# Gate, up and query rows in half the width, the mean after the MLP from sums of w_down's rows, and a new order of loads for a two-layer decode step

## The chip, the cores and the metric

The kernel runs on one core of a Trainium2 chip. The metric is the device time of one execution in microseconds. Shown are the median of three runs and one profiled execution with its trace.

## The reference

One decode step for four tokens through attention, a gated MLP, and both once more with the same weights and the same caches.

```python
def _A_ref(x, k_cache, v_cache, wq, wo):        # x (4, 1, 512); caches (4, 8, 4096, 128)
    q = (x @ wq) as 32 heads of 128
    k, v = each of the 8 cached heads for 4 query heads
    p = softmax(q @ k.T * 128 ** -0.5)
    return (p @ v) as one row of 4096 @ wo
def _B_ref(x, w_gate, w_up, w_down):            # (512, 1792), (512, 1792), (1792, 512)
    return (sigmoid(x @ w_gate) * (x @ w_up)) @ w_down

x = A_x
x = x + _A_ref(_layernorm(x), A_k_cache, A_v_cache, A_wq, A_wo)
x = x + _B_ref(_layernorm(x), B_w_gate, B_w_up, B_w_down)
x = x + _A_ref(_layernorm(x), A_k_cache, A_v_cache, A_wq, A_wo)
x = x + _B_ref(_layernorm(x), B_w_gate, B_w_up, B_w_down)
```

All inputs are bf16. K and V of one token and all 8 heads are 8.4 MB each, 67 MB for four tokens, and both layers need them; the ring below holds 14.7 MB of them at a time.

## The kernel before

**Units and half tiles.** The work is cut into 16 units `bhl`: token b, half hg of the 8 cached heads (four heads s), layer l. A unit reads 8 half tiles of K and 8 of V, each 512 KB: one head s, one half q of the 4096 positions. SBUF has a ring of 28 slots (`SLOTS`), each for one half tile. `UNITS` gives the order of the units: `000 010 011 100 001 110 200 111 210 101 211 300 310 201 311 301`. Layer 1 of a token can start only when both of its layer-0 units are done and the token has passed its MLP.

**Loads.** `LOADS` is the order of all loads on SP's queue, written out: a word is a weight (`wq0`, `wo3`, `wg`) or K or V, the unit, and a letter: `a` to `d` a head's both halves in one transfer of 1 MB into two neighbouring slots, `e` to `h` its first half, `i` to `l` its second half, a digit two single halves. A half tile of layer 1 that LOADS doesn't name is kept: the tile of layer 0 stays in its slot until layer 1 has used it. Before, 80 of the 128 half tiles of layer 1 are kept: 23 of token 0, 21 of token 1, 16 of token 2, 20 of token 3. A load waits until the readers of its slot's last tile are done; the wait stands on SP's queue, in order, so the loads behind it wait too.

**A unit.** K tiles are transposed in place on DVE (L896), then PE makes the scores (L904) in `S_ps`. `unit_probs` makes the softmax: maximum on DVE (L928), exponential on ACT (L949), a transpose (L955), 16 products that turn the probabilities (L960), copies to `pt_sb` (L970). `unit_values` multiplies with V (L1003), copies the result (L1025, L1033), adds the parts up (L1056), scales into `oT` (L1078, L1082). In layer 0 PE then multiplies with w_o (L1108).

**The chain of a token.** Between its layers each token has a chain of small steps (`chain`). `gate_up` multiplies one row of x with w_gate and w_up (L1217): 4 column groups of 448 in 4 strips of the array. `gated` makes the tanh on ACT (L1249), the gated product (L1258) and its transpose (L1268) on DVE, in two cuts (`CUTS`: 4 and 10 of 14 pieces of 32 columns). `down` multiplies with w_down, 56 products (L1288). Two DVE steps add the result to x (L1321). The mean of x is a product with a constant (L1330), its copy (L1333), the variance (L1335, L1197), and `rstd` on POOL (L1205). `gated` keeps its values in the slot of a tile that layer 1 loads anew (`LENT`, one word for each chain), which is held from the tanh to the last down product.

**The queries of layer 1** (`queries`) multiply x, which still has its mean in it, with w_q (L826): 16 products of 512 columns, four rows in `Q_ps`. ACT copies them (L835), 4 products turn them (L840), DVE takes off the mean times the column sums of w_q (L846), 16 products on the unit matrix spread them into the scores' layout (L855), DVE masks them into `zq` (L869). `column_sums` makes these sums once (L783, L792).

**The end.** The last unit's w_o product (L1438) and MLP are made for all four tokens at once (`last_part`, `last_chain`), with cuts of 6, 2 and 6 pieces (`LAST_CUTS`); the up product's second part goes to `O_ps`.

**The order on the engines.** All steps are put into a `_Plan`. `schedule` walks through time with a cost for each step, a rank (the load's place, moved by `SHIFTS` for each stage) and a model of the load queue (`DMA_RATE`, `DMA_LAG`, `DMA_SPREAD`), and so gives each engine a fixed order and each load its slot. Where PE would idle it puts constant products in between (`filler`, L1553). The device follows that order, whatever its own times are.

Of the kernel before, what the change touches and what calls it, by code (L numbers as in the profile page):

```python
# [5 lines left out]
dt = mybir.dt  # L6
# [11 lines left out]
DMA_LAG = 1.4  # L18
DMA_SPREAD = 0.2
DMA_START = 1.9  # L20
PATIENCE = 6.201
# [9 lines left out]
CUTS = "0 4 14"  # L31
LAST_CUTS = "0 6 8 14"
PAIRS = "02"
GROUPS = "1441441444214244"
HEADS = "2212222122222222"
LENT = "V00031 V20030 V10110 V21111 V20110"
CHAIN = -3108.651
PROJECT = 2584.665
KEPT_K = -953.257
KEPT_V = -2637.133  # L40
REST_V = 88.299
SHIFTS = {'c0': 81.66, 'c2': -0.1, 'd1': -11.9, 'd2': -26.55, 'd3': 76.83, 'm0': 8.0, 's': 77.55, 'z0': -0.3, 'z16': 4.38, 'z8': 30.04, 'z12': 50.86, 'q0': -15.2, 'v0.1': 92.64, 'o0.1': -4.74, 'w0.1': 248.14, 'k1.0': 4.46, 'p1': 45.85, 'k2.0': -9.73, 'k2.1': -29.77, 'v2.0': -5.96, 'o2.1': -101.79, 'd0': 5.31, 'q3': 51.38, 'k3.1': -52.81, 'p3': 23.58, 'v3.1': -25.26, 'k4.0': -0.08, 'k4.1': 17.87, 'p4': 24.28, 'v4.1': -24.56, 'k5.0': 19.47, 'k5.1': 3.74, 'p5': -17.71, 'v5.0': -8.59, 'v5.1': 34.03, 'w5.1': -6.54, 'p6': -80.04, 'o6.0': -17.29, 'w6.1': -3.83, 'k7.1': 8.14, 'v7.1': -5.26, 'o7.1': -29.48, 'k8.0': -34.2, 'k8.1': 17.95, 'p8': 6.04, 'v8.0': 9.7, 'o8.0': -79.15, 'v8.1': -48.83, 'p9': -1.07, 'v9.1': -42.81, 'o9.1': 15.12, 'w9.1': 1.54, 'k10.1': 20.55, 'v10.0': -41.15, 'o10.0': 9.85, 'w10.0': 36.93, 'w10.1': -3.91, 'k11.0': 7.83, 'k11.1': 36.1, 'v11.0': -4.55, 'v11.1': -2.06, 'k12.1': 314.91, 'v12.0': -16.87, 'o12.0': 1.68, 'w12.0': -0.97, 'q13': 19.97, 'k13.0': 8.85, 'k13.1': -1.52, 'p13': 139.58, 'o13.0': 113.53, 'o13.1': 4.81, 'q14': 42.47, 'k14.1': 1.8, 'p14': -41.58, 'v14.1': 15.08, 'o14.1': 8.19, 'k15.0': 1.08, 'p15': 22.58, 'v15.1': -5.53, 'o15.1': 8.17, 'end': 93.62, 'm1': -11.57, 'k9.0': 3.6, 'w9.0': -21.96, 'k14.0': -6.21, 'c1': 140.82, 'k1.1': 22.57, 'g0': 4.64, 'p2': 0.84, 'o3.1': 18.77, 'v6.0': 2.8, 'v6.1': 0.53, 'q7': -42.76, 'v7.0': 20.84, 'v9.0': -119.56, 'n2': 30.1, 'w11.1': 12.47, 'v13.0': -0.64, 'm3': -25.74, 'v14.0': -1.05, 'k0.1': -45.97, 'p0': 102.93, 'q1': 2.86, 'v1.0': -18.16, 'w3.1': -27.61, 'q5': 12.61, 'w5.0': 9.87, 'g1': -13.65, 'k7.0': 3.96, 'q8': -81.66, 'w8.0': -3.75, 'w8.1': -1.25, 'k9.1': 0.11, 'm2': -13.04, 'q10': -18.43, 'p11': -11.23, 'w11.0': -1.15, 'w12.1': 6.19, 'k0.0': 68.44, 'q2': 66.34, 'v2.1': -36.47, 'v4.0': -8.75, 'o5.0': 32.07, 'o6.1': -88.15, 'h2': 12.76, 'k10.0': -23.93, 'o10.1': -2.79, 'o11.0': -25.41, 'o12.1': 30.81, 'h3': 13.66, 'q15': 3.29, 'o15.0': 2.09, 'z24': -1.06, 'o0.0': -6.06, 'o1.0': 5.71, 'w1.0': 9.25, 'v3.0': -6.6, 'o3.0': -26.33, 'o4.0': -29.01, 'k6.0': 37.29, 'o8.1': -47.34, 'k12.0': 6.65, 'p12': 57.66, 'v12.1': -18.06, 'w0.0': -12.21, 'v1.1': 68.17, 'o1.1': 38.85, 'n0': 10.09, 'h0': 9.25, 'o5.1': -51.91, 'k6.1': 42.17, 'h1': -4.92, 'p7': 48.17, 'o7.0': -24.25, 'o9.0': -10.3, 'g2': 1.73, 'p10': -2.59, 'q11': -13.05, 'v13.1': 117.04, 'g3': 39.19, 'o14.0': -0.78, 'v15.0': 19.07}
PUT_OFF = -380.691
UNITS = "000 010 011 100 001 110 200 111 210 101 211 300 310 201 311 301"
LOADS = "V000a V000d V010g wq1 K010b V010b K000d K000a wq0 V010k K000b wo1 K010a K010k V000c K000c V010a K010g K010d wu V000b wo3 wo0 V010d wo2 wg wd K100g K100h V011j K011j K100l V100e K100i K001a K100e K100b K001d K100k V001f K110d V100i V100b V100d K110c K110b K110a V001d V100k K200d K200c V100g K200a K200b V110e V110i V110b V110d V110c V200c V200h V200l V2000 V2001 K210l K210k K210g K210a V111l K210h K101g K101d K210b V210b K101e V210a K300c V210d V210c V101j V101i V101d V101g V101k K300b K310a K310c K300a K300d V300a K201e K310b K310d V300c V300d V300b V310b V310a V310c V310d K201f K201h K301g K201g K201j K201i K2013 V201i V201f V201e V201j K301f V201c K301k V201d V311d V301e V301b V301c V301h V301l"
# [389 lines left out]
def bass_interleave_layers__gqa_block_cached__glu_gated_glu__decode_kernel(nc, A_x, A_k, A_v, A_wq, A_wo, B_x, B_wg, B_wu, B_wd, out):  # L435
# [14 lines left out]
    FB = FS // 32  # L450
    TH = T // 2
# [52 lines left out]
    small = sb_low("small", [P, 76], bf)  # L504
    xT = small[:, 0:16].rearrange("p (b k) -> p b k", b=B)
    q2, sel = small[:, 16:32], small[:, 32:36]
    sel_o = small[:, 40:72].rearrange("p (t n) -> p t n", t=4)
    ob = q2
    real = sb("real", [P, 80])
    stat = sb_low("stat", [P, 24])  # L510
    col_sum = sb_low("col_sum", [P, 2 * HG])
    mean_of = sb_low("mean_of", [P, B])
    minus = sb_low("minus", [P, 2], bf)[:, 0:1]
    more = sb_low("more", [P, 25])
# [59 lines left out]
    S.put("pool", lambda e: e.memset(minus, -1.0), writes=["minus"], cost=0.1)  # L574
    const("sel", sel, 0.0, [(sel, NE, 1.0, 0, [[-32, 4]])])
# [10 lines left out]
    const("sel_o", small[:, 40:72], 0.0, [  # L586
# [127 lines left out]
    def rank_v(u, pr):  # L714
# [19 lines left out]
        reads=["ones"] + [f"xsum{b}" for b in range(B)], writes=["U", "Uz"], cost=0.35, pairs=2,  # L734
    )
    less_b = U_ps[:, 0:4].unsqueeze(2).broadcast_to([P, B, KD])
    for o, key in ((xT, "xT"), (xc, "xc")):
# [8 lines left out]
        reads=["ones"] + [f"xsq{b}" for b in range(B)], writes=["U"], cost=0.35, pairs=2,  # L746
# [29 lines left out]
    def column_sums(hg):  # L776
        S.stage = f"c{hg}"
        r = max(place["wq0"], place["wq1"]) + 25.0
        for c0 in range(0, HG, 4):
            fns = []  # L780
            for c in range(c0, c0 + 4):
                for k in range(KD):
                    fns.append(lambda e, c=c, k=k: e.matmul(  # L783
                        Q_ps[:, c * WIDE:(c + 1) * WIDE], lhsT=wq[:, k, hg * HC + c * DH:hg * HC + (c + 1) * DH],
                        rhs=minus.broadcast_to([P, WIDE]), start=(k == 0), stop=(k == KD - 1),
                    ))
            S.put(
                "pe", fns, reads=["wq0", "wq1", "Qz", "minus"], writes=[own("Q", c0 == 0)], rank=r, columns=len(fns) * 4 * WIDE,
                lock="Q" if c0 == 0 else None,
            )  # L790
        S.put(
            "dve", lambda e: e.tensor_copy(col_sum[:, hg * HG:(hg + 1) * HG], Q_ps[:, bass.ds(0, HG, step=WIDE)]),  # L792
            reads=[own("Q")], writes=[f"cs{hg}"], cost=0.2, rank=r, free="Q",
        )

    q_out = Q_ps[:, 0:64].rearrange("p (s n h) -> p s n h", n=NQ, h=R)

    def queries(i, rank):
# [797 lines left out]
```

## Time and profile before

| | |
|---|---|
| median of three runs | 285.12 us (284.92 to 286.09) |
| profiled execution | 282.97 us |
| its span, first to last instruction | 281.1 us |
| busy: PE, DVE, ACT, POOL | 217.4, 174.0, 63.5, 10.7 us |
| read from HBM | 106.17 MB |
| load queue on SP | 106.18 MB in 115 K and V transfers and 9 of weights |
| mean granted TensorE clock | 0.988 |

In the rows of the profile an instruction group reads: line, engine, operation, written tile <- read tiles, shapes, count | busy us, mean ns of one | idle time of the engine before them and what ended it. `SPq` rows are issues on the load queue; a wait of SP names the instruction whose end let the load go. PE's busy time holds the constant products.

### The profile page before, as it was taken

To read this page: it belongs to the slowest core of one execution; us is meant where nothing else is said; L and a number is where in the kernel's file an instruction comes from. 1 tells how busy PE (TensorE), PEld (TensorE's weight loads), DVE (VectorE), ACT (ScalarE), POOL (GpSimd) and SP (SyncE) were. 2 spreads that over 40 slices of the span, in tenths; PEclk is the share of its full clock that TensorE was granted. 3 is DMA by queue.
4 is the path that set the end of the run, shared out by engine and by line. 5 is a ranking of instruction groups with operands and counts; after the bars stand their busy time and mean duration, and the time that the engine had idled before them with its cause. 6 is when DMAs were issued, how large, how long until landed. Compare 5 with 4: busy or idle time off the path is not lost.

```text
span 281.1 us, 8157 instructions
## 1 busy us (share of the span) xinstructions
PE 217.4 (77%) x3572; PEld 112.2 (40%) x3612; DVE 174.0 (62%) x387; ACT 63.5 (23%) x155; POOL 10.7 (4%) x40
## 2 busy tenths in 40 slices
PE   1000786988889688999889886898889789989796
PEld 1000444444543343434355441355424454544464
DVE  4036379747268897858623788635999517975222
ACT  1000100052122105002132240332132312233611
POOL 5200000000000000000000000000000000000000
PEclk9999997999999999999999997999999999999999
DMA  7999999999998999999999999999999999989910
GB/s 266 429 422 426 385 417 417 411 380 397 420 369 322 417 385 427 415 416 418 420 412 387 354 419 423 415 413 422 419 417 419 423 408 366 349 293 404 421 61 3
DMA packets 21538, 106.69 MB, mean 380 GB/s; under 512 B 2048, under 2 KB 4096, under 8 KB 13056
## 3 DMA queue, kind: packets, MB, share of 16 engines
q1 hardware_dynamic: 21440, 106.18, 94.3%
q8 instruction: 28, 0.46, 0.7%
q14 instruction: 6, 0.05, 0.0%
q10 hardware_dynamic: 64, 0.01, 0.0%
HBM read 106.17 MB, written 0.00 MB: 378 GB/s over the span
## 4 chain that ended last, share of the span: by engine, by line
DMA 50%; PE 27%; DVE 10%; SPq 7%; issue 3%; ACT 1%; POOL 0%; ACTq 0%; DVEq 0%
DMA slots<-in_A_k_cache_dram 27%; DMA slots<-in_A_v_cache_dram 17%; PE S_ps L904 8%; DMA wd<-in_B_w_down_dram 7%; DVE slots L896 7%; SPq L659 4%; PE O_ps L1003 4%; PE G_ps L1288 2%; PE PT_ps L1553 2%; SPq L668 2%; PE G_ps L1553 2%; PE Q_ps L826 2%; PE M_ps L1056 1%; PE G_ps L1217 1%; PE M_ps L1349 1%
## 5 line engine op out<-in xcount | busy, mean ns | idle before, releaser
L896 DVE STREAM_TRANSPOSE slots<-slots 128x1024 int32<-128x1024 int32 x84 | 100.6, 1222 | 24.8 <-DMA slots<-in_A_k_cache_dram 24.0
L904 PE MATMUL S_ps<-slots,zq 128*32 128x512 bf16 x512 | 62.0, 401 | 7.5 <-DVE slots L896 5.3
L1003 PE MATMUL O_ps<-slots,pt_sb 128*16 128x512 bf16 x504 | 35.9, 380 | 6.2 <-DMA slots<-in_A_v_cache_dram 4.0
L1553 PE MATMUL PT_ps<-wq 128*128 128x512 bf16 (+1 forms) x123 | 33.8, 378 | 2.9 <-issue 2.7
L904 PEld LDWEIGHTS S_ps<-slots,zq 128*32 128x32 bf16 x512 | 19.7, 96 | 35.2 <-DVE slots L896 11.5
L1033 ACT ACTIVATE slots<-O_ps 128x512 bf16<-128x512 f32 (+1 forms) x26 | 15.5, 595 | 47.7 <-PE O_ps L1003 47.7
L760 PE MATMUL Q_ps<-small,wq 128*128 128x4 bf16 x128 | 3.6, 165 | 22.8 <-DMA wq<-in_A_wq_dram 22.8
L1553 PEld LDWEIGHTS PT_ps<-wq 128*128 128x128 bf16 x155 | 12.5, 98 | 19.7 <-issue 12.1
L1003 PEld LDWEIGHTS O_ps<-slots,pt_sb 128*16 128x16 bf16 x504 | 10.6, 87 | 18.3 <-ACT pt_sb L970 4.4
L1108 PEld LDWEIGHTS M_ps<-oT,wo 128*128 128x128 bf16 x512 | 14.7, 97 | 6.5 <-DVE oT L1082 2.9
L1108 PE MATMUL M_ps<-oT,wo 128*128 128x32 bf16 x512 | 16.0, 176 | 1.1 <-DVE oT L1082 0.7
L928 DVE TENSOR_REDUCE small<-S_ps 128x1 f32<-128x512 f32 x16 | 11.0, 687 | 8.7 <-PE S_ps L904 5.6
L970 ACT ACTIVATE pt_sb<-PT_ps 128x256 bf16<-128x256 f32 x32 | 10.5, 381 | 13.0 <-PE PT_ps L960 12.8
L1205 POOL TENSOR_TENSOR stat<-real,small 128x1 f32<-128x1 f32 x8 | 4.4, 549 | 233.1 <-ACT real L1201 233.1
L760 PEld LDWEIGHTS Q_ps<-small,wq 128*128 128x128 bf16 x128 | 3.5, 100 | 23.3 <-DMA wq<-in_A_wq_dram 22.9
L1056 PE MATMUL M_ps<-small,slots 128*64 128x4 bf16 (+2 forms) x204 | 9.7, 176 | 2.8 <-DVE oT L1082 1.3
L1056 PEld LDWEIGHTS M_ps<-small,slots 128*128 128x128 bf16 (+1 forms) x204 | 7.1, 103 | 11.4 <-issue 5.0
L1553 PE MATMUL G_ps<-wq 128*128 128x512 bf16 (+1 forms) x35 | 11.0, 435 | 0.6 <-issue 0.3
L949 ACT ACTIVATE p_sb<-S_ps,pt_sb,stat 128x512 bf16<-128x512 f32 x8 | 7.5, 935 | 16.5 <-DVE pt_sb L942 13.2
L770 ACT ACTIVATE oT<-Q_ps 128x64 bf16<-128x64 f32 x2 | 0.9, 448 | 43.5 <-PE Q_ps L760 43.5
L955 DVE STREAM_TRANSPOSE p_sb<-p_sb 128x256 int32<-128x256 int32 x16 | 7.0, 439 | 5.3 <-ACT p_sb L949 5.2
L869 DVE TENSOR_TENSOR zq<-Q_ps,real 128x256 bf16<-128x256 f32 x16 | 6.4, 400 | 6.1 <-ACT oT L770 5.5
(146 smaller groups left out, 222.9 us busy)
## 6 DMA issues: line engine op xcount, KB each, us to landing
slots<-in_A_v_cache_dram SPq DMA_DIRECT2D x32, 1024.0 KB, 11.1
slots<-in_A_k_cache_dram SPq DMA_DIRECT2D x29, 1024.0 KB, 10.9
slots<-in_A_v_cache_dram SPq DMA_DIRECT2D x28, 512.0 KB, 11.8
slots<-in_A_k_cache_dram SPq DMA_DIRECT2D x26, 512.0 KB, 7.6
wq<-in_A_wq_dram SPq DMA_DIRECT2D x2, 2048.0 KB, 18.5
wo<-in_A_wo_dram SPq DMA_DIRECT2D x4, 1024.0 KB, 22.0
wu<-in_B_w_up_dram SPq DMA_DIRECT2D x1, 1792.0 KB, 23.9
wg<-in_B_w_gate_dram SPq DMA_DIRECT2D x1, 1792.0 KB, 17.0
```

What stands on the lines that cost most here:

```text
L659: return e.dma_start(o, src)
L760: fns.append(lambda e, c=c, k=k: e.matmul(Q_ps[:, c * B:(c + 1) * B], lhsT=wq[:, k, hg * HC + c * DH:hg * HC + (c + 1) * DH], rhs=xT[:, :, k],
L896: "dve", lambda e, t=t: e.transpose(ring[t.slot].bitcast(dt.int32), ring[t.slot].bitcast(dt.int32)),
L904: fns.append(lambda e, s=s, t=t, nn=nn, q=q: e.matmul(S_ps[qi][32 * s:32 * s + 32, :], lhsT=window(qi, s * NQ + nn, q), rhs=ring[t.slot].r ...
L928: dve(lambda e: e.tensor_reduce(ml[at], bank, AX.X, ALU.max, negate=True), [f"S{qi}s{s}" for s in ss], keys("ml", ss), 0.7)
L949: lambda e: e.activation(p_sb[at].rearrange("p (t j r) -> p t r j", j=32, r=2), bank.rearrange("p (t r j) -> p t r j", r=2, j=32), ACTF.Ex ...
L970: "act", lambda e, pr=pr: e.activation(pt_sb[:, (2 * i + pr) % 3], PT_ps[:, 256 * pr:256 * pr + 256], ACTF.Copy),
L1003: fns.append(lambda e, m=m, at=at, v=v, c=c, q=q, pt=pt, bank=bank, x0=x0, x1=x1: e.matmul(bank[m:m + 16, x0:x1], lhsT=pt[:, at:at + 16], ...
L1033: lambda e, lent=lent, rows=rows, o_ps=o_ps, rows_of=rows_of, cols=cols: e.activation(ring[lent.slot][rows, 0:cols], rows_of(o_ps[rows, 0: ...
L1056: return e.matmul(o, lhsT=turned[:, tt * P + at:tt * P + at + n], rhs=heads(tt), start=(tt == 0), stop=(tt == 3))
L1108: fns.append(lambda e, k=k, n=n, h0=h0: e.matmul(M_ps[:, k * WIDE:(k + 1) * WIDE], lhsT=wo[:, h0 + n, k * P:(k + 1) * P], rhs=oT[:, b, h0 ...
L1553: return lambda e: e.matmul(ps_of[:, 0:width], lhsT=wq[:, 0, 0:P], rhs=wq[:, 0, 0:width], start=True, stop=True)
```

## The change

Gate and up are made in two halves of the columns: 8 and 6 of the 14 pieces, stacked as two rows of each strip, so that the elementwise steps are 256 columns wide and not 448. The same is done with the query rows (two rows of 256 and not one of 512). For this x stands in `xz` with zeros on both sides, and each product takes two of the columns. The 4 products that turn the query rows and the 16 that spread them become 32 products that do both. x in `xT` now has its mean off already, by a sum over the gated values with the sums of w_down's rows (14 new reductions on DVE, `chain_sums`); `column_sums` goes. The mean's product stands inside the last cut's `down`, after two of its four groups. The variance is made on DVE (`squares`) and not on ACT. The planner's costs of some small steps change, as do its shifts, and LOADS, LENT, GROUPS and HEADS are new. The words of the new LOADS name 174 half tiles where there were 176, with token 0 keeping 25 where it kept 23; 54 loads are of 1 MB and 66 of 512 KB, where there were 61 and 54. The weights come in the order wo3 wq0 wq1 wo2 wo1 wo0 wd wg wu, where it was wq1 wq0 wo1 wu wo3 wo0 wo2 wg wd.

```diff
-DMA_LAG = 1.4
-DMA_SPREAD = 0.2
+DMA_LAG = 1.55
+DMA_SPREAD = 0.5
...
-CUTS = "0 4 14"
-LAST_CUTS = "0 6 8 14"
+CUTS = "0 2 8"
+LAST_CUTS = "0 4 8"
...
-GROUPS = "1441441444214244"
+GROUPS = "1421442441412144"
...
-LENT = "V00031 V20030 V10110 V21111 V20110"
+LENT = "K00001 V20020 V11101 K20130 V30120"
...
-LOADS = "V000a V000d V010g wq1 K010b V010b K000d K000a wq0 ... V010d wo2 wg wd K100g K100h V011j K011j K100l V100e ..."
+LOADS = "K010d K000d K000f K010j wo3 K010c wq0 K000c V000j K000a wq1 ... wo0 wd V010a V010k wg wu K100f K001i V100g K001j K100d ..."
...
 # queries, layer 1
             for k in range(KD):
                 fns = []
                 for s in range(NS):
-                        fns.append(lambda e, k=k, s=s: e.matmul(
-                            Q_ps[32 * s:32 * s + 1, :], lhsT=xT[:, b, k:k + 1], rhs=wq[:, k, hg * HC + s * 512:hg * HC + (s + 1) * 512],
-                            start=(k == 0), stop=(k == KD - 1),
+                    for a in range(2):
+                        fns.append(lambda e, k=k, s=s, a=a: e.matmul(
+                            Q_ps[32 * s:32 * s + 2, 0:256], lhsT=xz[:, b, k, 1 - a:3 - a],
+                            rhs=wq[:, k, hg * HC + s * 512 + 256 * a:hg * HC + s * 512 + 256 * a + 256],
+                            start=(k == 0 and a == 0), stop=(k == KD - 1 and a == 1),
                         ))
...
+            for nn in range(NQ):
+                for h in range(2):
+                    at = h * DH + 64 * (nn // 2) + nn % 2
+                    for a in range(0, P, 32):
+                        fns.append(lambda e, nn=nn, h=h, at=at, a=a: e.matmul(
+                            q_out[a:a + 32, :, nn, bass.ds(h, 2, step=2)], lhsT=p_sb[:, bass.ds(at, 32, step=2)], rhs=sel,
+                            start=True, stop=True,
+                        ))
...
 # gate_up
+            for a, end in ((0, c1), (1, min(c1, FB - FW))):
+                for j in range(4) if end > c0 else ():
+                    fns.append(lambda e, j=j, a=a, end=end: e.matmul(
+                        dealt(o_ps, (c0, end))[32 * j:32 * j + 2 * nb], lhsT=rows_of(k, a),
+                        rhs=w[:, k, j * FS:(j + 1) * FS].rearrange("p (i m) -> p i m", m=FB)[:, :, FW * a + c0:FW * a + end],
+                        start=(k == 0 and a == 0), stop=(k == KD - 1), skip_group_check=True,
+                    ))
...
 # chain, after the gated cuts
+        weighted(
+            lambda: turned(home).rearrange("p (m i) -> p m i", i=64)[:, :, 0:4], w_sums[:, 8:24].rearrange(pairs, r=4),
+            ..., part_sum[:, 1:2],
+            [f"th{home.name}cd{c0}" for c0, c1 in cuts(CUTS)] + ["wd_sums"], ["part1"], rank,
+        )
+            down(
+                cut, 1, G_ps, "G", rank, home,
+                (lambda: mean_part(U_ps[:, 1:2], part_sum[:, 1:2], ["part1"], rank, True, True)) if cut[1] == FW else None,
+            )
+                out=rest1, in0=U_ps[:, 1:2].broadcast_to([P, KD]), scalar=rs, in1=xc1, op0=ALU.mult, op1=ALU.subtract
...
 # chain_sums
-        for key, at, count, rows in (("wo", 0, 8, lambda n: wo[:, H - 8 + n, :]),):
+        for key, at, count, rows in (("wo", 0, 8, lambda n: wo[:, H - 8 + n, :]), ("wd", 8, FB, lambda n: wd[:, n, :])):
...
 # last_part
+            "pool", lambda e: e.memset(small[:, 0:48], 0.0), writes=[f"xT{b}" for b in every_b], cost=0.1, rank=rank - 4.0,
```

More of the change, by code (lines that the diff above doesn't have):

```diff
@@ L774, in first_q @@
         )
[L776 to L794, printed above, removed]
     q_out = Q_ps[:, 0:64].rearrange("p (s n h) -> p s n h", n=NQ, h=R)
@@ L876, in queries @@
             ),
[L877 removed]
+            reads=[own("Q"), by_key], writes=[f"qz{qi}"], cost=0.41, rank=rank, free="Q",
         )
```

235 lines of the change are left out of this document (108 added, 127 removed).

## The prediction

> **What bounds the kernel now.** I read the page's head, the DMA part and the shares of the chain that ended last; then a table of windows for the rate of the load stream; then, where the rate is low, SP's queue and the chain.
>
> ```profile
> span 281.1 us, 8157 instructions
> q1 hardware_dynamic: 21440, 106.18, 94.3%
> DMA 50%; PE 27%; DVE 10%; SPq 7%; issue 3%; ACT 1%; POOL 0%; ACTq 0%; DVEq 0%
> ```
>
> The load queue moved 106.18 MB and was busy for 94.3% of the span, and half of the last chain is DMA. The kernel is a stream of loads with a tail behind it. The windows show where the stream ran thin (columns: length, busy time of PE, PEld, DVE, ACT, POOL, granted clock, DMA share, GB/s).
>
> ```profile
> 10.00:30.00 20.00, 0.46 (x17) 0.46 (x18) 7.11 (x6) 0.00 (x0) 0.00 (x0) 1.00 1.01 423
> 105.00:130.00 25.00, 22.50 (x263) 9.90 (x264) 18.47 (x31) 5.34 (x13) 0.00 (x0) 1.00 1.01 421
> 60.00:80.00 20.00, 16.98 (x323) 9.44 (x319) 9.83 (x32) 5.08 (x12) 0.55 (x1) 1.00 1.03 404
> 75.00:90.00 15.00, 13.63 (x198) 6.43 (x201) 9.47 (x19) 2.94 (x9) 1.10 (x2) 1.00 0.92 347
> 150.00:160.00 10.00, 8.66 (x194) 5.06 (x185) 5.87 (x15) 3.09 (x9) 0.61 (x2) 1.00 0.97 353
> 235.00:255.00 20.00, 18.22 (x309) 8.80 (x309) 16.41 (x41) 6.55 (x19) 1.10 (x2) 1.00 0.92 331
> 267.50:281.10 13.60, 11.10 (x238) 7.56 (x239) 4.03 (x20) 2.53 (x7) 0.55 (x1) 1.00 0.06 21
> ```
>
> An undisturbed stretch runs at 421 GB/s. Against that, 75 to 90 us lacks 15 x 74 = 1.11 MB, which is 2.6 us of loading; 150 to 160 lacks 0.68 MB, 1.6 us; 235 to 255 lacks 1.80 MB, 4.3 us. These are the stretches of the chains of tokens 0, 1 and 3: while a token is between its layers, its kept tiles hold their slots. The loads end near 267.5 us and 13.6 us of tail follow.
>
> So three things move the end: the bytes, the three dry spells, and the tail.
>
> The first dry spell: SP's waits and issues, two windows of 1 us, and the chain there (start, us, what):
>
> ```profile
> SPq L427 <- PE G_ps L1288: 13.2, 1, 13.2
> 64.56 1.18 SPq L659 DMA_DIRECT2D slots<-in_A_k_cache_dram  x2
> 65.84 0.52 SPq L659 DMA_DIRECT2D slots<-in_A_v_cache_dram  x1
> 66.40 14.91 SPq L659 DMA_DIRECT2D slots<-in_A_k_cache_dram  x2
> 84.54 0.33 SPq L659 DMA_DIRECT2D slots<-in_A_v_cache_dram  x1
> 85.24 4.60 SPq L659 DMA_DIRECT2D slots<-in_A_k_cache_dram  x6
> ...
> 85.00:86.00 1.00, 0.98 (x17) 0.33 (x16) 1.00 (x2) 0.00 (x0) 0.00 (x0) 1.00 0.53 82
> 86.00:87.00 1.00, 0.98 (x20) 0.33 (x16) 1.00 (x2) 0.00 (x0) 0.00 (x0) 1.00 0.91 369
> 60.24 18.97 DMA wd<-in_B_w_down_dram
> 79.35 1.56 PE G_ps L1288 x56
> 85.18 1.13 PE S_ps L904 x14
> ```
>
> Behind w_d (landed by 79.3) four half tiles were issued by 66.4; the next waited 13.2 us for the first chain's down products, whose lent tile held the slot. These four are the 28 slots less 23 kept halves of token 0 less the lent one. The next came at 84.5, after the first scores of unit 100 had freed a slot, and a row of six from 85.2, as layer 1's first scores (85.18) began; the stream ran at 82 GB/s from 85 to 86 and at 369 in the next us, so data flows some 1.5 us after an issue.
>
> **The change, part by part.** The prices are in these rows and the ones behind them.
>
> ```profile
> L896 DVE STREAM_TRANSPOSE slots<-slots 128x1024 int32<-128x1024 int32 x84 | 100.6, 1222 | 24.8 <-DMA slots<-in_A_k_cache_dram 24.0
> L1382 DVE TENSOR_REDUCE more<-wo x8: 676/686/687, 62.6 to 68.4; 128x1 f32<-128x512 bf16 x8
> L783 PE MATMUL Q_ps<-minus,wq 128*128 128x32 bf16 x128 | 3.5, 176 | 3.1 <-DVE col_sum L792 3.1
> L970 ACT ACTIVATE pt_sb<-PT_ps 128x256 bf16<-128x256 f32 x32 | 10.5, 381 | 13.0 <-PE PT_ps L960 12.8
> L835 ACT ACTIVATE p_sb<-Q_ps 128x512 bf16<-128x512 f32 x8 | 4.8, 598 | 15.4 <-PE Q_ps L826 13.7 <-PE PT_ps L960 1.8
> L1258 DVE SCALAR_TENSOR_TENSOR p_sb<-slots,U_ps 128x128 bf16<-128x128 f32 x4 | 1.1, 280 | 7.4 <-ACT slots L1249 7.4
> L1258 DVE SCALAR_TENSOR_TENSOR p_sb<-slots,U_ps 128x320 bf16<-128x320 f32 x4 | 1.9, 484 | 0.0
> L1258 DVE SCALAR_TENSOR_TENSOR p_sb<-slots,stat,O_ps 128x192 bf16<-128x192 f32 x1 | 0.4, 377 | 0.0
> L1268 DVE STREAM_TRANSPOSE slots<-p_sb 128x64 int32<-128x64 int32 x4 | 1.2, 291 | 0.1
> L1268 DVE STREAM_TRANSPOSE slots<-p_sb 128x160 int32<-128x160 int32 x4 | 1.8, 456 | 0.1
> L1268 DVE STREAM_TRANSPOSE slots<-p_sb 128x96 int32<-128x96 int32 x2 | 0.7, 349 | 0.0
> ```
>
> *Bytes.* The words of LOADS sum to 176 half tiles before and 174 after. A half is 0.524 MB, at 421 GB/s 1.25 us: two save 2.5 us of loading. Both are kept by token 0 (23 kept become 25; the others stay at 21, 16 and 20).
>
> *What that takes from the first chain.* With 25 kept and one lent, 2 slots are left instead of 4. Cover behind the last weight falls from four transfers to two, 2.5 us less. The last weight is now w_up, not w_d, with the same bytes ahead of it (30.7 MB), so it lands at the same 79.3. Behind it come the up products, the gating and the last 40 down products, where before there were 56 down products: up 0.93, first cut 0.28 + 0.23, second 0.38 + 0.35, 40 x 26 ns = 1.1, hand-overs 0.3, so about 3.6 against 1.6 us. The queries that follow are about 0.9 shorter (below). So layer 1's first scores come at about 86.3 instead of 85.2. My timeline: two halves last until 81.8; the lent slot is freed near 83.2 and, 1.5 us later, data flows at 84.7; that half and one in a slot freed by unit 100's first scores last to 87.2; the next slots come free near 87.0 and flow at 88.5. That is 2.9 + 1.3 = 4.2 us dry where the window had 2.6: 1.7 us more, rounding up. Ends: nothing, if unit 100's tiles turn over faster; 3.5 us (the two lost transfers and 1 us of later scores), if no slot of unit 100 comes free early. I take 1.7, nearer the row that shows a slot of unit 100 coming free at 84.54.
>
> *Narrow gate, up and queries.* A chain's columns on PE stay the same (448 become 256 + 192, in twice the matmuls). The elementwise steps shrink: the cuts of 128 and 320 columns become 64 and 192, so the products go from 280 + 484 to about 280 + 377 ns and the transposes from 291 + 456 to about 233 (the rows' slope) + 349 ns, 0.27 us together. The copy of the query rows falls from 598 to the 381 ns of a 256-wide copy, 0.22 us.
>
> The up products and the query's way to the scores' layout (token 1):
>
> ```profile
> 149.29 0.93 PE L1217 MATMUL U_ps<-wu,small 128*1 128x448 bf16 x16
> ...
> 154.66 0.38 PE L1330 MATMUL U_ps<-stat 128*128 128x1 f32 x2
> 155.51 0.26 PE L840 MATMUL Q_ps<-small,p_sb 128*128 128x4 bf16 x4
> 155.88 0.23 DVE L846 SCALAR_TENSOR_TENSOR small<-col_sum,mean_of,Q_ps 128x16 bf16<-128x16 f32 x1 [2.02 <-PE Q_ps L840]
> 156.29 0.27 PE L855 MATMUL Q_ps<-small,ident 128*32 128x16 bf16 x16
> ```
>
> From 155.51 to 156.56 are 1.05 us with two hand-overs. 32 products of L855's form replace them: 16 took 0.27, of which 0.17 is the latency of one, so 6.7 ns each, and 32 take 0.38. That saves 0.67. Against that, the mean's two matmuls (0.31 of issue; L1330's pair, which stood after or among the query rows) now stand inside the down products, ahead of x. Twice the matmuls cost some 0.14. A chain is 0.27 + 0.22 + 0.67 - 0.31 - 0.14 = 0.7 us shorter. Chain 0 has this counted above. Chain 2 has no dry spell. Chains 1 and 3 have 1.6 and 4.3 us dry, and I take 0.5 of each: K transposes of 1.22 us sit ahead of the chain's steps on DVE and will eat some. Ends: 0 and 1.4 for both.
>
> [...]
>
> *w_d sums.* 14 reductions of L1382's 686 ns, 9.6 us of DVE, behind w_d, which now lands near 66.7 (5.3 MB ahead of the last weight). DVE was busy 9.83 of 20 us from 60 to 80, of which L1382's w_o sums took 5.5 between 62.6 and 69; these move early, as w_o's last quarter is now the fifth load (DVE has 7.11 busy of 20 between 10 and 30). From 66.7 to 80.8, when the gated products need them, there are 14 us with some 3 busy. I cost them at nothing; three fewer K tiles are transposed (3.7 us). If the cover is gone, x waits for the mean, and each us late is a us dry: 0 to 2.
>
> *Column sums.* 128 products on PE (3.5 us) and two copies go, ahead of the first chain, which waits for its weights: nothing. The loads now begin with K, and the second half of w_q lands after 12.1 MB instead of 11.0: the first products start 2.6 us later under a full load queue, nothing, up to 1 if slots then run short. Twelve more single-half transfers add issue time on SP, which runs ahead: nothing, up to 0.3. The extra memsets on POOL stand ahead of their uses: nothing.
>
> *The tail.*
>
> ```profile
> 274.95 0.39 PE U_ps L1217 x16
> 275.75 0.41 DVE L1258 SCALAR_TENSOR_TENSOR p_sb<-slots,stat,U_ps 128x192 bf16<-128x192 f32 x1 [1.17 <-ACT slots L1249]
> 276.89 1.55 PE L1288 MATMUL G_ps<-slots,wd 128*128 128x32 bf16 x56
> ```
>
> Gating began at 275.75 and the first down product came at 276.89, after the transposes of the first two cuts. With cuts of 128 columns: product 0.28, transpose 0.29, so down starts near 276.35, and its 56 products run on without a gap (the second cut ends near 276.95, the first one's 32 products near 277.2). That is 0.55 us earlier; ends 0 and 0.7.
>
> *Sum.* The profiled execution took 282.97 (281.1 in the span, 1.9 around it): 282.97 - 2.5 + 1.7 - 1.0 - 0.55 = 280.6. The median shown, 285.12, is 2.15 above that execution, so 282.8 for the median.
>
> **Rivals.**
> *More than forecast.* The first dry spell doesn't grow: 282.8 - 1.7 = 281.1, to 280.7 with all of both chains' 0.7. For it: slots of unit 100 did come free during the chain. Against: half the free slots are gone. 0.18.
>
> *The gain is eaten where it is made.* The first spell grows by 3.5: 284.6, the same. For it: 13.2 us of SP's wait there hung on one lent slot. Two transfers saved cost two transfers of cover. [...]
>
> *Slower: w_d's sums late.* The sums end after the first chain's gating. xT now waits for the mean, so each us late is a us more dry. It is the same beyond 0.9 us late (283.7) and slower beyond 3.8 (286.6); all 9.6 us behind the gating would give 292. DVE's 10 idle us from 60 to 80 speak against it. 0.07.
>
> *Slower: the new order itself.* Every load and step has a new place. A new spell as long as the one at 235 to 255 (4.3 us) would give 287.1; it decides from 3.8. 0.12. The profile can't show it.
>
> **How the numbers follow.** About 0.5% (1.4 us) can be told from no change, so faster ends at 283.7 and slower begins at 286.5. Forecast 0.38, and 0.18 for more: faster 0.56. Same: 0.25. Slower: 0.19. For 8 in 10 the range runs from 279.8 (the fuller gain with 0.7 more where the new order closes part of 235 to 255) to 286.8; the forecast's own is 281.1 to 283.7.
>
> **What would show it.** The load queue at 105.1 MB. 75 to 90 us thinner than 347 GB/s (about 300), with SP waiting for L1288 or first scores behind two halves; 150 to 160 and 235 to 255 fuller by 0.5 us each. The 32 products in about 0.4 us. From the last load to the end 13 us. Wrong if the first spell is not thinner, if the mean's matmuls wait for w_d's sums, or if a stretch that is full now runs dry.

## The result, and the profile after

The changed kernel takes 288.09 us (median of 17 runs, 286.18 to 290.72) where the kernel before, run beside it, takes 285.30 (283.66 to 286.46): a ratio of 1.0087, 95% interval 1.0065 to 1.0110. (The ratio leaves out the two slow executions of the changed kernel, 290.56 and 290.72: it is 287.79 over 285.30.) It is slower; faster by 2.3 us was forecast. The profiled execution took 286.65 us, its span 284.4 against 281.1: 3.3 us more. The page's head, the load queue and the shares of the chain that ended last:

```profile
span 284.4 us, 8832 instructions
q1 hardware_dynamic: 22160, 105.13, 92.2%
PE 41%; DMA 38%; SPq 8%; DVE 7%; issue 3%; ACT 2%; ACTq 0%; DVEq 0%
```

The queue moved 1.05 MB less, as planned, and was busy for a smaller share of a longer span. Loads are 38% of the last chain where they were 50%: more time is waited for something else. Windows of the changed kernel, in the columns used above, the last one the tail:

```profile
75.00:95.00 20.00, 19.34 (x416) 12.00 (x420) 11.90 (x41) 3.08 (x11) 1.10 (x2) 1.00 0.65 237
80.00:82.00 2.00, 2.00 (x41) 1.02 (x37) 0.00 (x0) 0.90 (x3) 0.56 (x1) 1.00 0.22 88
86.00:88.00 2.00, 1.84 (x57) 1.04 (x46) 1.21 (x2) 0.45 (x2) 0.55 (x1) 1.00 0.79 256
150.00:165.00 15.00, 13.13 (x330) 8.58 (x332) 4.95 (x27) 2.72 (x8) 1.10 (x2) 1.00 0.88 333
230.00:255.00 25.00, 24.04 (x459) 14.23 (x463) 16.98 (x45) 4.79 (x13) 1.05 (x2) 1.00 0.98 381
271.70:284.40 12.70, 10.12 (x272) 7.56 (x268) 3.33 (x18) 2.27 (x6) 0.55 (x1) 0.95 0.04 12
```

and three of the same windows of the kernel before:

```profile
75.00:95.00 20.00, 16.59 (x251) 7.80 (x254) 12.83 (x25) 5.16 (x14) 1.10 (x2) 1.00 0.94 364
150.00:165.00 15.00, 13.17 (x281) 7.51 (x272) 9.97 (x26) 4.40 (x13) 0.61 (x2) 1.00 0.99 374
230.00:255.00 25.00, 22.75 (x377) 11.16 (x378) 18.40 (x47) 7.15 (x20) 1.10 (x2) 1.00 0.94 345
```

Each spell is (421 less the rate) times the length over 421. The first, of chain 0, was 20 x 57 / 421 = 2.7 us and is 20 x 184 / 421 = 8.7: 6.0 us more. Chain 1's went from 1.7 to 3.1, 1.5 more before rounding. Chain 3's went from 4.5 to 2.4, 2.1 less. With 2.5 us for the bytes and 0.5 for the tail (from 267.9 to the end it was 13.2 us, from 271.7 it is 12.7) this makes 6.0 + 1.5 - 2.1 - 2.5 - 0.5 = 2.4 of the 3.3 us. Of the rest, 0.4 us is already there at 80 us (395 GB/s over the first 80 us, where it was 397); the remainder lies spread over the other stretches.

So nearly all of the loss is in one place. There SP's queue shows (start, us):

```profile
50.16 0.50 SPq L668 DMA_DIRECT2D wd<-in_B_w_down_dram  x1
60.25 0.81 SPq L659 DMA_DIRECT2D slots<-in_A_v_cache_dram  x2
61.10 0.43 SPq L668 DMA_DIRECT2D wg<-in_B_w_gate_dram  x1
61.58 0.51 SPq L668 DMA_DIRECT2D wu<-in_B_w_up_dram  x1
62.18 14.53 SPq L659 DMA_DIRECT2D slots<-in_A_k_cache_dram  x2
85.05 0.33 SPq L659 DMA_DIRECT2D slots<-in_A_v_cache_dram  x1
87.30 5.16 SPq L659 DMA_DIRECT2D slots<-in_A_k_cache_dram  x7
```

and its transfers issued from 55 to 80 us (size, time from issue to landing):

```profile
wu<-in_B_w_up_dram SPq DMA_DIRECT2D x1, 1792.0 KB, 18.0
slots<-in_A_v_cache_dram SPq DMA_DIRECT2D x1, 1024.0 KB, 9.1
slots<-in_A_v_cache_dram SPq DMA_DIRECT2D x1, 512.0 KB, 10.0
```

w_up landed at 61.58 + 18.0 = 79.6. The two V transfers issued from 60.25 on are the last values of unit 010, V010a and V010k; the first landed at 60.25 + 9.1 = 69.35, the second near 70.7. Before, token 0's last values were issued at 54.83 and landed 12.9 us later, at 67.7 (queue, transfer, and then a step on DVE):

```profile
54.83 2.55 SPq L659 DMA_DIRECT2D slots<-in_A_v_cache_dram  x1
```

```profile
slots<-in_A_v_cache_dram SPq DMA_DIRECT2D x1, 1024.0 KB, 12.9
```

```profile
73.92 0.16 DVE L1125 TENSOR_TENSOR small<-M_ps,more 128x4 bf16<-128x4 f32 x1 [0.18 <-PE M_ps L1108]
```

The last row is x of token 0 as it is written into `xT`, at 73.92. In the changed kernel that is L1088, and chain 0 goes on from it; DVE's row and then PE's:

```profile
78.51 0.16 DVE L1088 TENSOR_TENSOR small<-M_ps,more 128x4 bf16<-128x4 f32 x1
```

```profile
67.03 4.26 PE L1544 MATMUL PT_ps<-wq 128*128 128x512 bf16 x19
71.22 1.04 PE L966 MATMUL O_ps<-slots,pt_sb 128*16 128x512 bf16 x16
78.77 0.81 PE L1189 MATMUL G_ps<-wg,small 128*2 128x256 bf16 x24
80.14 1.25 PE L1544 MATMUL PT_ps<-wq 128*128 128x512 bf16 x5
81.32 1.02 PE L1189 MATMUL U_ps<-wu,small 128*2 128x256 bf16 x32
...
87.16 0.37 PE L809 MATMUL Q_ps<-small,p_sb 128*32 128x8 bf16 x32
...
88.12 1.14 PE L867 MATMUL S_ps<-slots,zq 128*32 128x512 bf16 x16
```

The first products with the late values (heads 0 and 1; V010a is head 0) run at 71.22. V010a had landed 1.9 us before; PE, which follows its fixed order, was still at 19 constant products. x is ready at 78.51 (4.6 us later than before), the gate products start at once, five constant products follow them, the up products come at 81.32, 1.7 us after w_up's landing, and layer 1's first scores at 88.12, where they came at 85.18. By the two windows of 2 us above, the stream runs dry near 80.4 and flows again after 86.

### The profile page after: what moved, and what is told of

It reads as the page before. It is cut to its first block, busy times and chain, and to the rows that moved or that the text cites. A ratio compares the mean times of both kernels' runs of the same rounds, so it can differ in the third digit from the quotient of the medians.

```text
span 284.4 us, 8832 instructions
## 1 busy us (share of the span) xinstructions
PE 225.5 (79%) x3903; PEld 124.4 (44%) x3945; DVE 177.3 (62%) x406; ACT 58.8 (21%) x142; POOL 10.9 (4%) x42
## 3 DMA queue, kind: packets, MB, share of 16 engines
q1 hardware_dynamic: 22160, 105.13, 92.2%
## 4 chain that ended last, share of the span: by engine, by line
PE 41%; DMA 38%; SPq 8%; DVE 7%; issue 3%; ACT 2%; ACTq 0%; DVEq 0%
DMA slots<-in_A_k_cache_dram 20%; DMA slots<-in_A_v_cache_dram 10%; PE S_ps L867 9%; DMA wo<-in_A_wo_dram 7%; SPq L659 7%; PE PT_ps L1544 7%; PE O_ps L966 5%; DVE slots L859 4%; PE G_ps L1266 3%; PE M_ps L1071 2%; PE Q_ps L791 2%; PE M_ps L1019 2%; PE G_ps L1189 2%; PE G_ps L1544 1%; PE U_ps L1189 1%
## 5 line engine op out<-in xcount | busy, mean ns | idle before, releaser
L859 DVE STREAM_TRANSPOSE slots<-slots 128x1024 int32<-128x1024 int32 x81 | 96.7, 1222 | 16.9 <-DMA slots<-in_A_k_cache_dram 16.4
L1544 PE MATMUL PT_ps<-wq 128*128 128x512 bf16 (+1 forms) x191 | 50.0, 378 | 3.0 <-issue 2.4
L867 PEld LDWEIGHTS S_ps<-slots,zq 128*32 128x32 bf16 x512 | 21.3, 99 | 34.4 <-DVE slots L859 13.3
L1544 PEld LDWEIGHTS PT_ps<-wq 128*128 128x128 bf16 x225 | 19.2, 99 | 24.9 <-issue 9.1
L1045 DVE TENSOR_TENSOR oT<-M_ps,real 64x8 bf16<-64x8 f32 x32 | 5.1, 158 | 12.0 <-PE M_ps L1019 11.8
L912 ACT ACTIVATE p_sb<-S_ps,pt_sb,stat 128x512 bf16<-128x512 f32 x8 | 7.5, 931 | 14.2 <-DVE pt_sb L905 12.9
L912 ACT ACTIVATE p_sb<-S_ps,pt_sb 128x512 bf16<-128x512 f32 x8 | 6.6, 829 | 15.2 <-DVE pt_sb L905 12.6
L1372 DVE TENSOR_REDUCE more<-wd 128x1 f32<-128x512 bf16 x14 | 9.6, 684 | 0.3
## 6 DMA issues: line engine op xcount, KB each, us to landing
slots<-in_A_v_cache_dram SPq DMA_DIRECT2D x28, 1024.0 KB, 12.7
```

The costliest lines, as they stand in the source:

```text
L859: "dve", lambda e, t=t: e.transpose(ring[t.slot].bitcast(dt.int32), ring[t.slot].bitcast(dt.int32)),
L867: fns.append(lambda e, s=s, t=t, nn=nn, q=q: e.matmul(S_ps[qi][32 * s:32 * s + 32, :], lhsT=window(qi, s * NQ + nn, q), rhs=ring[t.slot].r ...
L912: lambda e: e.activation(p_sb[at].rearrange("p (t j r) -> p t r j", j=32, r=2), bank.rearrange("p (t r j) -> p t r j", r=2, j=32), ACTF.Ex ...
L1372: "dve", lambda e, n=n, to=to, rows=rows: e.tensor_reduce(w_sums[:, to:to + 1], rows(n), AX.X, ALU.add),
L1544: return lambda e: e.matmul(ps_of[:, 0:width], lhsT=wq[:, 0, 0:P], rhs=wq[:, 0, 0:width], start=True, stop=True)
```

## The experiments

Two theories at the start. *Cover:* token 0 keeps 25 half tiles, so two transfers less stand behind the last weight. *Chain:* layer 1's first scores come later, because w_up, and not w_d, is the last weight. The rivals: the sums of w_d's rows are in the way on DVE; the constant products between gate and up are.

**The kernel before, token 0 keeping 25.**

```diff
-LOADS = "... wo2 wg wd K100g K100h V011j K011j K100l ..."
+LOADS = "... wo2 wg wd K100g K100h K100l ..."
```

> The kernel before with two words less in its list of loads, V011j and K011j: token 0 keeps 25 halves as in the changed kernel, 174 halves are loaded, chain and weights as before. Slot theory: two transfers of cover are gone, so the spell between 75 and 95 us grows from 2.7 to 5.2 to 6.2 us and eats the 2.5 us of saved loading, ratio 1.000 to 1.004. Chain theory (the spell grew by the longer chain): layer 1's first scores stay at 85.2 and the spell grows by less than 1 us, ratio 0.991 to 0.995.

Ratio 1.0036 (1.0001 to 1.0071). The window from 75 to 95, and the down products of chain 0:

```profile
75.00:95.00 20.00, 17.27 (x257) 9.19 (x257) 10.86 (x23) 4.79 (x14) 1.10 (x2) 1.00 0.77 298
```

```profile
79.83 1.63 PE L1288 MATMUL G_ps<-slots,wd 128*128 128x32 bf16 x56 [0.88 <-DMA wd<-in_B_w_down_dram]
```

298 GB/s is a spell of 5.8 us, 3.1 more than before. The down products came 0.5 us later than before, so up to 0.5 of the 3.1 is a later chain. Two transfers of cover are worth 2.6 to 3.1 us of spell and save 2.5 us of loading: by itself this part of the change brings nothing.

**The kernel before, w_up last.**

```diff
+        sp[at["wu"]], sp[at["wd"]] = sp[at["wd"]], sp[at["wu"]]
+        up = [o for o in pe if o.stage == "g0" and "wu" in o.keys]
...
+        at = next(n for n, o in enumerate(pe) if o.stage == "d0")
+        pe[at:at] = up
```

> The kernel before, order and slots the same, with the loads of w_up and w_down exchanged, so that w_up is the last weight as in the changed kernel, and the first chain's up products moved on PE to just ahead of its down products. 23 halves kept, no sums. Chain theory: up and gating now follow the last weight, layer 1's first scores come at about 87.4 and not 85.2, the spell between 75 and 95 us grows from 2.7 to about 4.9 us, ratio about 1.008. Slot theory: four transfers still cover the chain, the spell grows by less than 1 us, ratio 1.000 to 1.003.

Ratio 1.0101 (1.0066 to 1.0135). The same window, one us of it, and the up products:

```profile
75.00:95.00 20.00, 16.25 (x237) 7.31 (x242) 10.53 (x22) 3.90 (x11) 1.11 (x2) 0.91 0.79 302
82.00:83.00 1.00, 0.98 (x36) 0.99 (x37) 0.00 (x0) 0.00 (x0) 0.00 (x0) 0.50 0.50 193
```

```profile
79.44 0.93 PE L1225 MATMUL U_ps<-wu,small 128*1 128x448 bf16 x16 [1.33 <-DMA wu<-in_B_w_up_dram]
```

The spell is 5.7 us, 2.9 more. The chain's first query products came at 83.63 and not at 81.22, 2.4 us later. A part of that may be the granted clock, which read 0.50 to 0.53 from 81 to 84, where the kernel before has 1.00. A chain that ends late costs about what it is late.

**Both at once.**

```diff
-LOADS = "... wo2 wg wd K100g K100h V011j K011j K100l ..."
+LOADS = "... wo2 wg wd K100g K100h K100l ..."
+        sp[at["wu"]], sp[at["wd"]] = sp[at["wd"]], sp[at["wu"]]
...
+        pe[at:at] = up
```

> The kernel before with both edits at once: token 0 keeps 25 half tiles (V011j and K011j out of LOADS), and w_up is loaded last, its products moved to just ahead of the first down product. Alone they lengthened the dry spell of chain 0 by 3.1 and 2.95 us. Theory A (two causes, each with its own part of the spell): 75 to 95 us at about 237 GB/s, a spell of 8.7 us, as the changed kernel shows, and a time of 288 to 290 us. Rival B (one cause, the longer one hides the other): about 300 GB/s, a spell of 5.8 us, and a time as in the two runs before, 288 us or less.

Ratio 1.0124 (1.0080 to 1.0168); the window moved

```profile
75.00:95.00 20.00, 15.97 (x243) 8.49 (x238) 9.48 (x21) 3.90 (x11) 1.11 (x2) 1.00 0.69 252
```

which is 8.0 us: 5.3 more than before, of the 6.0 that the two give alone. Cover lost and lateness add up; neither hides the other. Here the clock stayed at 1.00, the query products came 2.1 us later than before (83.31), and w_up's place adds 5.3 - 3.1 = 2.2. In the changed kernel the same two terms would be 3.1 us for the cover and 2.9 for the scores (88.12 for 85.18), together the 6.0 measured; that is a sum and no run of its own. It leaves open what makes the chain late in the changed kernel itself.

**The changed kernel without the constant products between chain 0's gate and up products.**

```diff
+        # between the first and the last product of stage g0
+        self.prog["pe"] = [o for n, o in enumerate(pe) if not (first < n < last and o in fillers)]
```

> The changed kernel with the same order on every engine, but without the five constant products that stand on PE between the first chain's gate and up products. Chain theory (the first dry spell ends when token 0 reaches layer 1's first scores, and the constant products hold the up products back): the up products start near 80.2 us and not at 81.3, the first scores of layer 1 near 87.0 and not 88.1, the spell between 75 and 95 us shrinks from 8.8 by about 1.1 us, the ratio to before falls from 1.0087 to about 1.005. Slot theory (two fewer free slots set the spell, whatever the chain does): the up products move but the spell stays within 0.3 us and the ratio stays near 1.009.

Ratio to the kernel before 1.0069 (1.0037 to 1.0101). In this profile, as in the next two, the granted clock was 0.74 in 40 to 60 us, where that of the changed kernel shows 1.00, and chain 0's gate products began 0.8 to 1.3 us later; so chains are compared from the gate products on. PE's rows:

```profile
79.58 0.81 PE L1193 MATMUL G_ps<-wg,small 128*2 128x256 bf16 x24
80.84 1.02 PE L1193 MATMUL U_ps<-wu,small 128*2 128x256 bf16 x32
88.05 2.06 PE L871 MATMUL S_ps<-slots,zq 128*32 128x512 bf16 x32
```

From gate to scores it takes 8.47 us; with the constant products it took 88.12 - 78.77 = 9.35. They cost the chain 0.9 us. The window (233 GB/s) doesn't show it, since the chain began later here, and the ratio lies between the two forecasts, 1.005 and 1.009, with both in its interval. The up products no longer wait for anything but the gate's.

**The changed kernel with the sums over 32 of w_d's 512 columns** (a part of the mean is left out).

```diff
-        ... ("wd", 8, FB, lambda n: wd[:, n, :])):
+        ... ("wd", 8, FB, lambda n: wd[:, n, 0:32])):
```

> The changed kernel with the 14 sums of w_down's rows taken over 32 of the 512 columns, so that each takes about 0.15 us and not 0.69; part of the computation is left out (the mean after the MLP is wrong), order and waits are the same. Sums theory (9.6 us of DVE work ahead of the first chain delay token 0): the gate products start 1 us or more earlier than 78.8, and the spell and the ratio fall by as much. Chain and slot theories: the gate products may start up to 0.5 us earlier, but the up products still come behind w_up and the constant products, the first scores stay within 0.3 us of 88.1, and the ratio stays near 1.009.

Ratio 1.0099 (1.0062 to 1.0135), 222 GB/s in the window. DVE was 6.9 us less busy from 60 to 80 (4.48 for 11.38) and nothing came earlier: the gate products began at 79.67, where they began at 79.58 in the run above. From the first products with the late values to the gate products it takes 7.54 us in both runs (from 72.13 and 72.04), and 7.55 in the changed kernel. The sums were hidden.

**The changed kernel with w_up and w_d exchanged.** The sums are left out (zeros stand for them), as are the constant products of the run above.

```diff
+        sp[at["wu"]], sp[at["wd"]] = sp[at["wd"]], sp[at["wu"]]
+        self.prog["pe"] = [o for n, o in enumerate(pe) if not (first < n < last and o in fillers)]
...
+        self.prog["dve"] = [o for o in dve if o not in sums]
```

> The changed kernel with w_up and w_d exchanged on the load queue, so that w_d lands last, the sums of w_d's rows left out (zeros stand in their place, so the mean after the MLP is left out of the result), and the constant products between the gate and the up products of chain 0 taken out; all other constant products stay, and V010a and V010k stay behind the first weight. Theory A (in the changed kernel two things hold chain 0 back side by side, w_up's landing near 79.6 and the late values of unit 010, which make x ready at 78.5; either alone is enough): x at 78.5 as before the edit, the up products behind the gate at 80.1 and not 81.3, the scores at 87.0 where the changed kernel has 88.1, 75 to 95 us near 260 GB/s, a time 1 us shorter. Rival B (the order of the weights is the whole loss of the chain): scores near 85.2, 75 to 95 us near 300 GB/s, a time 3 us shorter, 285 us.

Ratio 1.0076 (1.0043 to 1.0110), 234 GB/s from 75 to 95. x on DVE, and the chain on PE:

```profile
79.32 0.17 DVE L1100 TENSOR_TENSOR small<-M_ps,more 128x4 bf16<-128x4 f32 x1
```

```profile
80.04 0.81 PE L1201 MATMUL G_ps<-wg,small 128*2 128x256 bf16 x24
81.31 1.03 PE L1201 MATMUL U_ps<-wu,small 128*2 128x256 bf16 x32
88.51 2.06 PE L879 MATMUL S_ps<-slots,zq 128*32 128x512 bf16 x32
```

From gate to scores 8.47 us, to the hundredth what it takes with w_up last. So the order of the weights, which costs 2.2 to 2.9 us in the kernel before, costs nothing here: x comes too late for it to matter. The scores missed both forecasts, 87.0 and 85.2: the gate products began 1.3 us later in this profile; less that, they are at 87.2. The second theory falls in its form: in the kernel before, w_up last is enough to make the chain late; in the changed one the late x stands in front of it.

**The last values ahead of w_d** (the constant products of 65 to 85 us and the full sums taken out; the narrow sums put behind the layer norm).

On SP the order wd V010a V010k wg wu becomes V010a V010k wd wg wu:

```diff
+        part = [o for o in part if o.sem not in named] + [named[k] for k in 'wd wg wu'.split()]
+        sp[at:late + 1] = part
...
+        self.prog["pe"] = [o for n, o in enumerate(pe) if not (mid - 20 <= n < end and o in fillers)]
...
+        dve[at:at] = wd
```

> The changed kernel, with V010a and V010k issued ahead of w_d, the constant products between the scores' last values and the first down product taken out, and the sums of w_d's rows over 32 of 512 columns (a part of the result is left out by that) and put behind the layer norm on DVE, so that they don't stand in the way. w_up stays last. Theory A (in the changed kernel w_up last and the late values of unit 010 each cost chain 0): x is ready near 75 and not 78.5 us, the up products start when w_up lands, near 79.6 and not 81.3, the scores come near 86.4 and not 88.1, 75 to 95 us moves about 273 GB/s and not 237, and the time falls by 1.7 us. Rival B (w_up alone sets the chain): scores stay within 0.5 us of 88.1 and the window below 250 GB/s. Rival C (the order of the steps on DVE sets it): x isn't earlier than 77.

Ratio 1.0305 (1.0244 to 1.0366). A window of 2 us around the issue of the values, DVE's row of x, and PE's rows:

```profile
60.00:62.00 2.00, 1.92 (x35) 0.87 (x28) 0.33 (x2) 0.60 (x1) 0.00 (x0) 1.00 0.37 112
```

```profile
74.17 0.17 DVE L1103 TENSOR_TENSOR small<-M_ps,more 128x4 bf16<-128x4 f32 x1
```

```profile
77.66 1.29 PE L1204 MATMUL G_ps<-wg,small 128*2 128x256 bf16 x24 [3.80 <-DMA wg<-in_B_w_gate_dram]
82.19 1.66 PE L1204 MATMUL U_ps<-wu,small 128*2 128x256 bf16 x32 [2.25 <-DMA wu<-in_B_w_up_dram]
```

x was ready at 74.17, so rival C falls, and the sums alone don't do that (without them, in the run before this one, x came at 79.32). But this run takes two things off the way to x at once: the first values landed at 60.86 + 5.2 = 66.1 and not at 69.35, and the 19 constant products ahead of their products are gone. Wherever these constant products stayed, the products with the values began right behind them: at 71.22, 72.04, 72.13 and 72.43 in the changed kernel and the three runs above, each time without idle time of PE before them; in the changed kernel V010a had landed 1.9 us before. In that order earlier values alone would not have made them start sooner. So theory A's x near 75 holds, and its cause, the late values, is not shown. The planner puts constant products where it expects PE to idle, so the late loads may be why they stand there; that is argued. The rest of A's numbers missed by far (194 GB/s from 75 to 95), and rival B is not tested by them. SP waits for the slot of V010a until 60 us in both orders; with w_d behind that wait the queue ran empty (112 GB/s from 60 to 62) and w_gate and w_up landed 2.5 us later (75.1 and 79.6 in the changed kernel). The other two edits came with costs of their own: the moved sums, 3.0 us from 84.75 on, stood ahead of the mean, and without constant products the granted clock fell to 0.50 (0.57 over 75 to 95), and 24 gate products took 1.29 us for 0.81.

**The same with the weights as before, w_d last.**

```diff
-        part = [o for o in part if o.sem not in named] + [named[k] for k in 'wd wg wu'.split()]
+        part = [o for o in part if o.sem not in named] + [named[k] for k in 'wu wg wd'.split()]
```

> As the run with the early values (V010a and V010k first, no constant products there, narrow sums put behind, which leaves out a part of the result), but with the weights in the order of the kernel before: w_up, w_gate, w_d last. Theory A (w_up last is the cause of some 2 us of the chain): gate and up products by 77, the down products when w_d lands, near 79.8, the scores near 85 where the run with the early values has 86.4, 75 to 95 us near 300 GB/s, and a time 3 us below the changed kernel, 285 us. Rival B (the order of the weights is worth nothing once the values are early): scores as in that run, 86.4, and the same window.

Ratio 1.0202 (1.0155 to 1.0249), 212 GB/s from 75 to 95. Layer 1's first scores came after 92 (`zq`, which they read, was written on DVE from 91.61 to 92.03), since the same faults are in it; it tells only that it is 1.0% faster than the run with w_up last. Whether w_up's place costs when x is early is not settled by this pair, as the granted clock differs too (0.66 over 75 to 95 for 0.57).

**The changed kernel with cover given back:** V011j and K011j loaded behind w_up. Other loads change places too (V010k now stands ahead of w_d, wo0 behind it), and the planner's ranks, shifts and LENT are set anew.

```diff
-LOADS = "... V010g wo0 wd V010a V010k wg wu K100f K001i ..."
+LOADS = "... V010g V010k wd wo0 V010a wg wu V011j K011j K100f K001i ..."
```

> The changed kernel with two loads put back behind w_up (V011j and K011j, so token 0 keeps 23 half tiles, 1.05 MB more to read) and the planner's ranks and shifts set anew for this list, so the order of some steps differs throughout. Theory A (the two lost transfers of cover are worth 3.1 us of the first spell): 75 to 95 us near 302 GB/s where the changed kernel has 237, and after 2.5 us for the two transfers a time 0.6 us shorter at best, 287 to 288 us. Rival B (the chain alone sets the spell's end, and the extra loads only move it): 75 to 95 us stays below 260 GB/s and the time rises to 290 us.

Ratio 1.0195 (1.0139 to 1.0251). Two windows:

```profile
75.00:95.00 20.00, 19.00 (x396) 11.25 (x398) 12.37 (x38) 3.18 (x10) 1.11 (x2) 1.00 0.64 237
80.00:85.00 5.00, 4.84 (x83) 2.54 (x77) 1.02 (x7) 0.92 (x3) 0.56 (x1) 1.00 0.59 234
```

From 80 to 85 the stream moved 234 GB/s, where it moved 35: the cover came back, 2.4 us of it. But the next row of K loads was issued at 90.17 and not at 87.30, so the spell was as long as ever, only later. The forecast of 302 GB/s missed. The chain was later too: its up products stand behind seven constant products (1.67 us from 81.40) and came at 83.00, where they came at 81.32. The new order has many differences, so this run doesn't tell which made the loads late, and what cover is worth in the changed kernel stays open.

**Chain 1.** In the changed kernel 16 products with unit 200's values stand between chain 1's up products and its tanh, and its spell grew. They were moved ahead of its gate products.

```diff
+        part = [o for o in pe if o.stage == "v6.1"]
...
+        at = next(n for n, o in enumerate(pe) if o.stage == "g1")
+        pe[at:at] = part
```

> The changed kernel with 16 products of unit 200 with its values (the 1.04 us of O_ps at 154.10, between chain 1's up products and its tanh) moved to just ahead of chain 1's gate products. SP's next loads wait for them. Theory A (these products, standing behind the gate and up products, lengthen the spell of chain 1 from 1.6 to 3 us): they end near 153, SP issues 1.5 us earlier, 150 to 165 us rises from 333 to about 365 GB/s, the tanh no longer waits for them, and the time falls by 1 us. Rival B (their values land only then, or the chain's own end sets the spell): the gate products wait for them, the scores come up to 1 us later than 161.5, 150 to 165 us stays within 10 of 333 GB/s, and the time doesn't fall.

Ratio 1.0160 (1.0113 to 1.0206), 303 GB/s from 150 to 165.

```profile
154.94 1.88 PE L972 MATMUL O_ps<-slots,pt_sb 128*16 128x512 bf16 x16 [1.88 <-DMA slots<-in_A_v_cache_dram]
156.61 1.33 PE L1195 MATMUL G_ps<-wg,small 128*2 128x256 bf16 x24
```

Rival B, and dearer than it said: PE waited 1.88 us for the values to land, and the whole chain behind them was later. They are late as loads; moving them there could gain nothing. What made chain 1's spell longer stays open, as does what made chain 3's shorter.

## Why the prediction was wrong

*Bytes:* right, 105.13 MB.

*The first dry spell:* the step that failed. The term was 1.7 us with an upper end of 3.5; it measured 6.0. Its timeline missed in three places. First, two K halves were to cover the stream until 81.8; it ran dry near 80.4. By the windows, only some 0.34 MB of their 1.05 MB were still to come when w_up landed. Second, the up products were to start as w_up lands, at 79.3, and the lent slot was to be free at 83.2, with data 1.5 us later. w_up landed at 79.6, but the up products began at 81.32: x came only at 78.51, so the gate products, which the timeline had as done, ran until 80.2, and five constant products stood behind them. From the up products to the scores it then took 6.8 us for a forecast of 7.0. The lent slot was free at 85.0, and the stream was dry until after 86. Third, from 88.5 on the timeline had a full stream; from 90 to 95 it moved 303 GB/s, where it moved 415 before.

What made x late is known in part. The diff puts V010a and V010k behind w_d, and they landed at 69.35 and near 70.7, where V010d landed at 67.7; and PE's order puts 19 constant products ahead of their first products, which ended 1.9 us after V010a's landing. I asked which weight comes last, and neither which values nor what PE does before them. Which of the two would be enough alone, no run shows.

The upper end was wrong for a second reason: it took 2.5 us for the cover, which the run of the kernel before bears out (2.6 to 3.1), and 1 us for later scores. The scores came 2.9 us later; with that this end would have been 5.4.

*The place of w_up:* it was priced at 2.0 us (3.6 behind the last weight and not 1.6), less 0.9 for shorter queries. In the kernel before, where the queries are as they were, the exchange made the query products 2.1 to 2.4 us later, so the price was about right. In the changed kernel the exchange shows nothing, since x came too late for it to matter.

*Chains 1 and 3:* 0.5 us each was taken for shorter chains. Chain 1 did get shorter, from x to the scores 0.5 us (10.23 to 9.75), and its spell still grew by 1.5; chain 3's shrank by 2.1, four times the term. That the two together come to 0.7 us less, for a forecast of 1.0, is luck. The elementwise prices were right, and the inference from a chain's length to its spell was not; what set these two spells stays open.

```profile
L1232 DVE SCALAR_TENSOR_TENSOR p_sb<-slots,U_ps 128x192 bf16<-128x192 f32 x4 | 1.4, 349 | 0.0
```

Forecast were 377 ns, and 233 for the transpose of 32 columns, which took 226; the copy of the query rows took 383 for 381. Twice the matmuls, 0.14 us in the sum, made the up products 1.02 us for 0.93.

*The 32 products:* 0.37 us for a forecast of 0.38. That is the row at 87.16 above.

*w_d sums, column sums:* nothing, as taken. *The tail:* 0.5 for 0.55.

*The rivals:* "Eaten where it is made" had the place right and the size too small. "Slower: the new order itself" had the sign, at 0.12, but looked for a new spell; it is the first one that grew, and the new order is part of that, by the constant products that it puts on chain 0's way. With 6.0 for 1.7 and the rest of the sum as it stood, 282.8 would have been 287.1, 1.0 below the measured median.

## What to carry to other kernels

A stall between two streams has a length of its own: the time from the last load that the chain needs to the first slot it frees, less the loads that stand ready behind it (in the changed kernel from 79.6 to 85.0, less the 0.34 MB still to come). Cover taken away and lateness added add up (5.3 of the 6.0 us that they cost alone), so a transfer saved by keeping a tile is no gain where it was covering such a stall (2.6 to 3.1 us of spell for 2.5 us of loading). To find when a chain starts, look for the last input of every kind in the load order, the activations' as well as the weights', for the slot wait ahead of which each one stands, and for the work that a fixed order puts on the engine ahead of the chain's first step.

## What was not expected of the hardware

The length of a gap on PE didn't tell whether the clock would fall. In the run with chain 1's products moved, PE stood for 1.88 us, from 153.06 to 154.94, and the granted clock read 0.50 in each window of 1 us from 155 to 158:

```profile
152.00:154.00 2.00, 1.06 (x28) 0.76 (x24) 0.78 (x6) 0.17 (x1) 0.00 (x0) 1.00 1.04 414
155.00:156.00 1.00, 1.00 (x12) 0.34 (x16) 0.00 (x0) 0.00 (x0) 0.00 (x0) 0.50 0.85 340
```

The 16 products behind the gap took 1.88 us for 1.04, and the gate products behind them 1.33 for 0.81. But in the kernel before PE stood for 1.86 us, from 93.69 to 95.55, and the clock read 1.00 in every us from 93 to 101. In the changed kernel it stood for 4.62 us, from 42.71 to 47.33, at 1.00 throughout and 1.00 over 40 to 60; in the run without the five constant products, which has the same order up to chain 0's gate products, the clock over 40 to 60 was 0.74. What decides between these is not shown. Five constant products taken out between gate and up made the chain 0.9 us shorter at full clock; with all of them taken out from 65 to 85 us PE stood for 3.80 and 2.25 us and the clock was at half.
